# Window attention and a gated product on one core: first product block by block, differences on VectorE, doubled scores behind the second product

## The chip, the core and the metric

The kernel runs on one core of a Trainium2 chip. TensorE (PE) multiplies, VectorE (DVE), ScalarE (ACT) and GpSimd (POOL) do the rest, and SyncE's queue (SP) issues every DMA. The metric is device time in microseconds (us) for the whole program. Before the change three runs gave 546.87, 548.37 and 548.40 us, median 548.37 us.

## The reference

```python
scores = 1/sqrt(64) * q @ k.T                      # 8 batches, 8 heads, 576 positions, 64 wide
scores = where(0 <= rel < 64, scores, -1e9)        # rel = query position - key position
attn   = exp(scores - max) / (sum + 1e-9)
x      = attn @ v                                  # heads side by side: 4608 x 512
h      = x @ w_in                                  # 512 x 1024
solu   = h * softmax(h)
ln     = (solu - mean) / sqrt(var + 1e-6) * g_ln
out    = ln @ w_out                                # 1024 x 512
```

The weights w_in and w_out arrive as 64-bit floats and are turned into 32-bit ones on the chip.

## The kernel before

The 4608 tokens are 36 tiles of 128. For each tile: scores (L400, one 64x128 block per head and half tile) into the one buffer pS; softmax (L428 and L433, or L421 on a masked tile; exponential L437, sums' reciprocal L446 and L449, scaling L452); the turn of the probabilities (PE transposes L506 and copies L511 for tiles 0 to 7, by DMA through memory, pd and raw, from tile 8); values (L530, into pX, copied to xH in L538 or L540 and its remainder xL in L541); the first product (L556 or L567, into the one buffer pH); the norm (maximum L582, exponential L584, product with its sum L587, square L593, power L600, scaling L604); the turn of that (L627, yd, L637, for tiles 1 to 33); the second product (L685 or L695, into pO) and the store (L702, L703).

Tiles 0 to 2 multiply plain 32-bit numbers in the first product, tile 0 in the second as well. Later tiles take three faster passes: rounded halves wH (made by ScalarE in L333) and remainders wL (L336). For both weights the remainder of a block's first half is made by VectorE and that of the second half by GpSimd. Each weight has four blocks (rows of 128 of w_in, of 256 of w_out): names w 0 to 3 and 4 to 7. L308 to L315 decode a block, L319 scales a block of w_out.

Masks: for tiles in MASKED (1 to 5) TensorE adds the mask to the scores by a 128x512 product with an identity (L384), VectorE takes two half maxima from PSUM (L421) and ScalarE's exponential reads PSUM. Other tiles get the mask on VectorE in L428, then a maximum in L433. SCALES = 3 is the first tile whose probabilities GpSimd scales, VectorE scaling the earlier ones. From tile EARLY = 3 VectorE copies the second half of the turned probabilities.

The order is written by a planner: each step states its engine, its cost, what it reads and writes. TensorE's steps stay in the order of the loop over t (L736 on), every other engine's steps are sorted by when TensorE's plan needs them. Where the plan has a gap on TensorE it puts products of the identity (L784, "filler", into pO). The buffers' counts (RINGS) set the remaining waits: one pH, one pS, nine weight slots "w", where eight hold the blocks and the remainders take over slots of blocks no longer needed.

In the loop, tile t's first product is followed by work for tiles ahead: scores of tile t+3 up to t = 3, and from t = 4 those of t+4; at t = 4 two sets of scores stand side by side (tiles 7 and 8). Tile t-3's second product closes the step from t = 3 on.

Of the kernel before, what the change touches and what calls it, by code (L numbers as in the profile page):

```python
# [24 lines left out]
NEG = -1.0e9  # L25

AHEAD = 3
FURTHER = 4

HASTE = 1  # L30
# [1 line left out]
LOOSE = 2  # L32
BEHIND = 3

EARLY = 3

JOINS = 8

PLANES = 4

HEADS = 1
MASKED = range(1, 6)
SCALES = 3

PLAIN_IN = 3
PLAIN_OUT = 1

BY_DMA = (1, 2)
# [137 lines left out]
def tile_window_attention_solu_moe(  # L186
# [17 lines left out]
    nc = tc.nc  # L204
# [7 lines left out]
    NC = DM // P  # L212
# [63 lines left out]
    def W32(i):  # L276
        return T("w", i, [P, 2, 512])
# [52 lines left out]
    def split(i):  # L330

        for x in range(2):
            plan.op("ACT", 600, lambda x=x: nc.scalar.copy(WH(i, x), W32(i)[:, x]),  # L333
                    [("w", i), ("w", i, x), ("w", NC + 1 if i < NC else NW - 1)], [("H", i, x)])
            engine, eng, cost = (("DVE", nc.vector, 690), ("POOL", nc.gpsimd, 1450))[x]
            plan.op(engine, cost, lambda x=x, eng=eng: eng.tensor_sub(  # L336
                WL(i)[:, x], W32(i)[:, x], WH(i, x).bitcast(F32)),
                [("w", i), ("w", i, x), ("H", i, x)], [("w", NW + i, x)])
# [37 lines left out]
    def scores(t):  # L376
        first = first_of(t)

        def emit():
            q, k = Q(t), K(t)  # L380
            if t in MASKED:
                mk = masksB[first]
                for r in range(2):
                    nc.tensor.matmul(  # L384
                        PS(t)[:, r], identB,
                        bass.AP(tensor=mk.tensor, offset=mk.offset, ap=[mk.ap[0], [0, NPAIR], mk.ap[1]]),
                        start=True, stop=False)
            for p in range(NPAIR):
                for half in range(2):
                    for r in range(2):  # L390
                        rs = slice(r * D, (r + 1) * D)
                        keys = k[rs, p, :P]
                        if half or first == 0:
                            a = k[rs, p, half * P:half * P + WIN]
                            gap = 0 if first == half else P
                            if half and gap:
                                a = k[rs, p, :WIN]
                            keys = bass.AP(
                                tensor=a.tensor, offset=a.offset, ap=[a.ap[0], [gap, 2], a.ap[1]])
                        nc.tensor.matmul(  # L400
                            PS(t)[half * WIN:(half + 1) * WIN, r, p],
                            q[rs, p, half * WIN:(half + 1) * WIN], keys, start=t not in MASKED,
                            stop=t not in MASKED or p == NPAIR - 1)

        plan.op("PE", 1430 if t in MASKED else 1000, emit, [("qk", t)], [("pS", t)], loose=t < LOOSE)
# [61 lines left out]
    def soft_planes(t):  # L467
        if t < SOFT_BY_DMA:
            return
        for x in range(2):  # L470
            engine, copy, cost = ("POOL", nc.gpsimd.tensor_copy, 1050)
            plan.op(engine, cost, lambda x=x, copy=copy: copy(  # L472
                PP(t)[:, :, 4 * x:4 * x + 4].rearrange("p k h n -> p k (h n)"),
                SS(t)[:, 4 * x:4 * x + 4].rearrange("p h n -> p (h n)").bitcast(U16).rearrange("p (n k) -> p k n", k=2)),
                [("sS", t, 4 * x + i) for i in range(4)], [(*SLOT(t)[0], x)])
# [41 lines left out]
    def XH(t):  # L517
        return T("xH", t, [P, NC, P], F32 if t < PLAIN_IN else F32R)
# [27 lines left out]
    def PH(t):  # L546
        return T("pH", t, [P, DFF], pool=ps_h)
# [4 lines left out]
    def moe_in(t, h):  # L552
        hs = slice(h * 512, (h + 1) * 512)
        if t < PLAIN_IN:
            for c in range(NC):
                plan.op("PE", 930, lambda c=c: nc.tensor.matmul(  # L556
                    PH(t)[:, hs], XH(t)[:, c], W32(c)[:, h],
                    start=(c == 0), stop=(c == NC - 1)),
                    [("xH", t), ("w", c), ("w", c, h)], [("pH", t)])
            return  # L560
        passes = [(c, *k) for c in range(NC) for k in (
            (XH, WH, "xH", "H", 0), (XH, WL, "xH", "w", NW), (XL, WH, "xL", "H", 0))]
        if t == PLAIN_IN:

            passes.sort(key=lambda k: k[4] == "w")
        for n, (c, x, w, xk, wk, o) in enumerate(passes):
            plan.op("PE", 233, lambda n=n, c=c, x=x, w=w: nc.tensor.matmul(  # L567
                PH(t)[:, hs], x(t)[:, c], WH(c, h) if w is WH else WL(c)[:, h],
                start=(n == 0), stop=(n == len(passes) - 1)),
                [(xk, t), (wk, o + c, h)], [("pH", t)])  # L570
# [108 lines left out]
    def moe_out(t):  # L679
# [22 lines left out]
        plan.op("ACT", 580, lambda: nc.scalar.copy(ot(), PO()), [("pO", t)], [("ot", t)])  # L702
        plan.dma(P * DM * 4, lambda: nc.sync.dma_start(out[t * P:(t + 1) * P, :], ot()), [("ot", t)], [])  # L703

    def on(f, t, *args):
        if 0 <= t < NTILE:
            f(t, *args)

    def ahead(t):

        at = t + AHEAD + (t >= FURTHER)
        return range(at - (t == FURTHER), at + 1)

# [22 lines left out]
    for t in range(NTILE + BEHIND):  # L736
        for a in ahead(t):
            on(load, a + 1)
        on(turn, t - 1)
        if t == PLAIN_IN:  # L740
            for i in range(NC):
                split(i)
        on(moe_in, t, 0)
        if t == 0:
            scores(2)
            softmax(2)
        if t < BEHIND:
            on(moe_in, t, 1)
            on(moe_norm, t)
            on(planes, t)  # L750
            on(transposes, t + 1)
            on(scores, t + AHEAD)
            on(softmax, t + AHEAD)
            on(soft_planes, t + AHEAD)
            on(soft_turn, t + AHEAD)
            on(join, t + 1)
            on(values, t + 1)
        else:
            on(transposes, t + 1)
            on(moe_in, t, 1)  # L760
            on(moe_norm, t)
            on(planes, t)
            if t - BEHIND < NTILE - BY_DMA[1]:
                on(moe_transpose, t - BEHIND)
            on(join, t + 1)
            on(values, t + 1)
            for a in ahead(t):
                on(scores, a)
                on(softmax, a)
                on(soft_planes, a)  # L770
                on(soft_turn, a)
            if t - BEHIND == PLAIN_OUT:
                for i in range(NC, NC + NF // 2):
                    split(i)
            if t - BEHIND + 1 >= NTILE - BY_DMA[1]:
                on(moe_transpose, t - BEHIND + 1)
            on(moe_out, t - BEHIND)

    plan.first = [("qk", 0), ("raw", 0), ("v", 0), ("qk", 1), ("raw", 1), ("raw", 2), ("raw", 3), ("v", 1), ("qk", 2)]
    def filler(n):  # L780
# [53 lines left out]
```

## Time and profile before

| | |
|---|---|
| runs | 546.87, 548.37, 548.40 us |
| profiled execution | 549.3 us, span from first to last instruction 547.5 us |
| PE busy | 530.9 us (97%) |
| DVE, ACT, POOL busy | 367.4, 330.3, 292.9 us |
| mean granted TensorE clock | 0.99 of full |
| DMA | 115.58 MB, mean 211 GB/s |

How to read it: PE is busy nearly all the time, so what the other engines do counts where PE waits. The page's line of the granted clock shows nines except one eight, in a slice of some 14 us. A busy PE can also be multiplying the filler, or running at the lower clock.

### The profile page before, as it was taken

The page shows a single profiled execution, that of the slowest core. Times are in us where ns is not written, and L with a number is a line of the kernel's source. Part 1 is how long each engine was busy: PE and PEld are TensorE (multiplying, and loading weights), DVE is VectorE, ACT ScalarE, POOL GpSimd, SP SyncE. Part 2 cuts the span into 40 slices and gives each one's busy share as a digit, 9 for nine tenths or more (in the row PEclk, how much of TensorE's full clock was granted, in tenths as well). Part 3 has the DMA queues.
Part 4 walks back from the last instruction along what each step waited for, and adds up shares of the span by engine and source line. Part 5 has one row for each costly group of instructions (what it writes and reads, how often), then busy time and mean ns, then how long its engine had stood idle before and what let it go on. Part 6 is the DMA issues. An engine that isn't in the chain of part 4 may idle for free.

```text
span 547.5 us, 11649 instructions
## 1 busy us (share of the span) xinstructions
PE 530.9 (97%) x4250; PEld 416.9 (76%) x4250; DVE 367.4 (67%) x725; ACT 330.3 (60%) x955; POOL 292.9 (53%) x490
## 2 busy tenths in 40 slices
PE   8799799899999999999999999999999999999996
PEld 7565486688877877778778777777877777777885
DVE  4999758766666666666666666666666677655530
ACT  4468475576666666666666666656666666663330
POOL 5214988664555555555555555555555555671110
PEclk9999989899999999999999999999999999999999
DMA  8963115647999999999999999999999994787211
GB/s 355 403 262 116 48 59 168 209 146 208 236 255 233 242 246 237 257 234 242 241 256 231 246 261 217 243 262 222 262 243 237 246 233 155 189 235 174 59 38 38
DMA packets 153081, 115.58 MB, mean 211 GB/s; under 512 B 129856, under 2 KB 129856, under 8 KB 152512
## 3 DMA queue, kind: packets, MB, share of 16 engines
q1 hardware_dynamic: 153024, 114.84, 81.0%
q8 instruction: 33, 0.54, 0.4%
q14 instruction: 24, 0.20, 0.1%
HBM read 41.42 MB, written 41.42 MB: 151 GB/s over the span
## 4 chain that ended last, share of the span: by engine, by line
PE 84%; DVE 7%; POOL 3%; issue 2%; DMA 2%; ACT 1%; SPq 0%; POOLq 0%; ACTq 0%
PE pO L695 35%; PE pH L567 33%; PE pX L530 6%; PE pS L400 5%; DMA raw<-pd 2%; DVE w L313 1%; PE pO L685 1%; DVE w L315 1%; PE pH L556 1%; POOL e L604 1%; DVE w L309 1%; PE t L506 1%; DVE sS L452 1%; POOL w L336 1%; POOL sS L452 1%
## 5 line engine op out<-in xcount | busy, mean ns | idle before, releaser
L452 POOL TENSOR_SCALAR sS<-sS,rec 128x128 f32<-128x128 f32 x264 | 117.4, 467 | 147.1 <-DVE rec L449 144.7
L695 PE MATMUL pO<-w_outH,yH 128*128 128x512 f32 x280 | 115.3, 412 | 0.7 <-ACT ot L702 0.7
L695 PE MATMUL pO<-w,yH 128*128 128x512 f32 x280 | 111.6, 399 | 0.0
L695 PE MATMUL pO<-w_outH,yL 128*128 128x512 f32 x280 | 110.6, 395 | 0.0
L567 PE MATMUL pH<-w_inH,xH 128*128 128x512 f32 x264 | 106.5, 403 | 0.0
L567 PE MATMUL pH<-w,xH 128*128 128x512 f32 x264 | 104.2, 398 | 0.0
L567 PE MATMUL pH<-w_inH,xL 128*128 128x512 f32 x264 | 104.1, 394 | 0.0
L437 ACT ACTIVATE sS<-sS,nmx 128x128 f32<-128x128 f32 x248 | 96.2, 390 | 9.6 <-DVE nmx L433 4.7
L702 ACT COPY ot<-pO 128x512 f32<-128x512 f32 x36 | 21.1, 587 | 97.8 <-PE pO L695 77.4
L584 ACT ACTIVATE e<-pH,mst 128x1024 f32<-128x1024 f32 x36 | 40.2, 1118 | 59.1 <-DVE mst L582 58.8
L582 DVE TENSOR_REDUCE mst<-pH 128x1 f32<-128x1024 f32 x36 | 44.1, 1224 | 42.0 <-PE pH L567 42.0
L604 POOL TENSOR_SCALAR e<-e,mst 128x512 f32<-128x512 f32 x72 | 60.1, 843 | 16.8 <-DVE mst L601 14.9
L596 DVE SCALAR_TENSOR_TENSOR mst<-mst 128x1 f32<-128x1 f32 x36 | 27.8, 772 | 60.1 <-ACT pl L593 60.1
L695 PEld LDWEIGHTS pO<-w_outH,yH 128*128 128x128 f32 x280 | 52.9, 189 | 18.0 <-issue 4.8
L695 PEld LDWEIGHTS pO<-w_outH,yL 128*128 128x128 f32 x280 | 53.0, 189 | 13.2
L695 PEld LDWEIGHTS pO<-w,yH 128*128 128x128 f32 x280 | 52.9, 189 | 10.9
L567 PEld LDWEIGHTS pH<-w_inH,xH 128*128 128x128 f32 x264 | 49.9, 189 | 13.2 <-ACT sS L437 0.2
L567 PEld LDWEIGHTS pH<-w_inH,xL 128*128 128x128 f32 x264 | 50.1, 190 | 12.4
L567 PEld LDWEIGHTS pH<-w,xH 128*128 128x128 f32 x264 | 49.6, 188 | 11.4 <-issue 0.2
L472 POOL COPY raw<-sS 128x1024 uint16<-128x1024 uint16 x56 | 56.7, 1043 | 0.0
L437 ACT ACTIVATION_READ_ACCUMULATOR sS<-sS,nmx 128x1 f32 x248 | 46.6, 188 | 0.0
L663 DVE TENSOR_TENSOR yL<-yT,yH 128x512 fp32r<-128x512 f32 x66 | 44.5, 708 | 2.6 <-ACT yH L661 2.6
(95 smaller groups left out, 867.0 us busy)
## 6 DMA issues: line engine op xcount, KB each, us to landing
qk<-qk SPq DMA_DIRECT2D x36, 640.0 KB, 5.9
yd<-pl SPq DMA_DIRECT2D x33, 512.0 KB, 6.6
pd<-raw SPq DMA_DIRECT2D x28, 512.0 KB, 3.7
v<-vS SPq DMA_DIRECT2D x36, 256.0 KB, 3.4
y<-ot SPq DMA_DIRECT2D x36, 256.0 KB, 3.1
raw<-w_in SPq DMA_DIRECT2D x4, 1024.0 KB, 10.6
raw<-w_out SPq DMA_DIRECT2D x4, 1024.0 KB, 8.6
yT<-yd SPq DMA_TRANSPOSE x33, 4.8
```

Of the source, the lines that this page charges most:

```text
L400: nc.tensor.matmul(PS(t)[half * WIN:(half + 1) * WIN, r, p], q[rs, p, half * WIN:(half + 1) * WIN], keys, start=t not in MASKED, stop=t no ...
L437: plan.op("ACT", 580, lambda h=h: nc.scalar.activation(SS(t)[:, h], PS(t)[:, h // NPAIR, h % NPAIR] if t in MASKED else SS(t)[:, h], AF.Ex ...
L452: plan.op(engine, cost, lambda h=h: v.tensor_scalar(SS(t)[:, h], SS(t)[:, h], rec()[:, h:h + 1], 0.0, ALU.mult, ALU.add), [("rec", t)], [( ...
L472: plan.op(engine, cost, lambda x=x, copy=copy: copy(PP(t)[:, :, 4 * x:4 * x + 4].rearrange("p k h n -> p k (h n)"), SS(t)[:, 4 * x:4 * x + ...
L530: nc.tensor.matmul(PX(t)[r * D:(r + 1) * D, p, ks], (V if half else VX)(t)[:, h * D:(h + 1) * D], PT(t)[:, r * NPAIR + p, ks], start=True, ...
L567: plan.op("PE", 233, lambda n=n, c=c, x=x, w=w: nc.tensor.matmul(PH(t)[:, hs], x(t)[:, c], WH(c, h) if w is WH else WL(c)[:, h], start=(n ...
L582: plan.op("DVE", 1230, lambda: nc.vector.tensor_reduce(nmax(), PH(t), axis=AX.X, op=ALU.max, negate=True), [("pH", t)], [key(0)])
L584: plan.op("ACT", 1320, lambda: nc.scalar.activation(E(t), PH(t), AF.Exp, bias=nmax(), scale=1.0, accum_out=se()), [("pH", t), key(0)], H2 ...
L596: plan.op("DVE", 130, lambda: nc.vector.scalar_tensor_tensor(kk(), se(), se(), ss(), ALU.mult, ALU.mult), [key(1), key(3)], [key(5)])
L604: plan.op("POOL", 770, lambda h=h, hs=hs: nc.gpsimd.tensor_scalar(E(t)[:, hs], E(t)[:, hs], nmean(), kk(), ALU.add, ALU.mult), [key(4), ke ...
L663: plan.op("DVE", 690, lambda hs=hs: nc.vector.tensor_sub(YL(t)[:, hs], YT(t)[:, hs], YH(t)[:, hs].bitcast(F32)), [("yT", t), ("yH", t, h)] ...
L695: plan.op("PE", 233, lambda f=f, i=i, x=x, k=k, y=y, w=w: nc.tensor.matmul(PO(), y(t)[:, f], w(i, x), start=(f == k == 0), stop=(f == NF - ...
```

## The change

TensorE's first product of tile 0 takes each block of w_in for both halves of the output before the next block (WIDE = 1). The remainders of w_in are all made by VectorE; those of w_out stay shared. Tiles 2 and 3 leave MASKED, so VectorE masks them. GpSimd scales from tile 2 on. ScalarE copies both halves of the turned probabilities of tile 3 too. The scores and softmax of tiles 2 to 5 get places from a table, and the second of the doubled scores stands behind the second product. The planner's price of a plain product falls from 930 to 870.

```diff
+PLACES = {2: (0, 0), 3: (0, 2), 4: (1, 2), 5: (2, 2)}
-EARLY = 3
+EARLY = 4
-MASKED = range(1, 6)
-SCALES = 3
+MASKED = (1, 4, 5)
+SCALES = 2
+WIDE = 1
@@ split
-            engine, eng, cost = (("DVE", nc.vector, 690), ("POOL", nc.gpsimd, 1450))[x]
+            engine, eng, cost = (("DVE", nc.vector, 690), ("POOL", nc.gpsimd, 1450))[x * (i >= NC)]
@@ moe_in
+            both = t < WIDE
+            if both and h:
+                return
             for c in range(NC):
-                plan.op("PE", 930, lambda c=c: nc.tensor.matmul(
-                    PH(t)[:, hs], XH(t)[:, c], W32(c)[:, h],
+                for x in range(2) if both else (h,):
+                    plan.op("PE", 870, lambda c=c, x=x: nc.tensor.matmul(
+                        PH(t)[:, x * 512:(x + 1) * 512], XH(t)[:, c], W32(c)[:, x],
...
+    def attend(t):
+        scores(t)
+        softmax(t)
+        soft_planes(t)
+        soft_turn(t)
+    def first_tiles(t, place):
+        for a, at in PLACES.items():
+            if at == (t, place):
+                attend(a)
@@ the loop
-        if t == 0:
-            scores(2)
-            softmax(2)
         if t < BEHIND:
+            first_tiles(t, 0)
             on(moe_in, t, 1)
             on(moe_norm, t)
             on(planes, t)
+            first_tiles(t, 1)
             on(transposes, t + 1)
-            on(scores, t + AHEAD)
...
+            first_tiles(t, 2)
...
-            for a in ahead(t):
-                on(scores, a)
...
+            for a in ahead(t)[:1]:
+                on(attend, a)
...
             on(moe_out, t - BEHIND)
+            for a in ahead(t)[1:]:
+                on(attend, a)
```

TensorE's order from the middle of tile 0's first product (pH_360; w_212, w_268, w_307 and w_341 are the blocks 0 to 3 of w_in; pS_402 before and pS_414 after are tile 2's scores, t the turned probabilities of tile 1). Before:

```order
L556 MATMUL pH_360<-w_341,xH_347 128x512
L384 LDWEIGHTS identB
L384 MATMUL pS_402<-maskNoneB,identB 128x512
L384 LDWEIGHTS identB
L384 MATMUL pS_402<-maskNoneB,identB 128x512
L400 MATMUL pS_402<-qk_165 64x128 x16
L556 MATMUL pH_360<-w_212,xH_347 128x512
L556 MATMUL pH_360<-w_268,xH_347 128x512
L556 MATMUL pH_360<-w_307,xH_347 128x512
L556 MATMUL pH_360<-w_341,xH_347 128x512
L506 MATMUL t_445<-ident,sS_314 128x128 x4
L506 MATMUL t_451<-ident,sS_314 128x128 x4
```

TensorE's rows at the same place now:

```order
L563 MATMUL pH_360<-w_212,xH_347 128x512 x2
L563 MATMUL pH_360<-w_268,xH_347 128x512 x2
L799 MATMUL pO_filler<-ident 128x128 x2
L563 MATMUL pH_360<-w_307,xH_347 128x512 x2
L799 MATMUL pO_filler<-ident 128x128 x2
L563 MATMUL pH_360<-w_341,xH_347 128x512 x2
L509 MATMUL t_400<-ident,sS_314 128x128 x4
L509 MATMUL t_407<-ident,sS_314 128x128 x4
L403 MATMUL pS_414<-qk_165 64x128 x16
```

Both products of a block stand together, nothing is left of the product behind the last block, and tile 2's scores come after tile 1's turn, without the mask.

VectorE's order around the maximum of tile 2's first product (mst_726 before, mst_683 after; w_673, w_706, w_716, w_760 before and w_675, w_731, w_758, w_769 after are the remainders of blocks 0 to 3; xL is tile 3's). Before:

```order
L336 TENSOR_TENSOR w_706<-w_268,w_inH 128x512
L592 RECIPROCAL mst_609<-mst_609 128x1
L336 TENSOR_TENSOR w_716<-w_307,w_inH 128x512
L582 TENSOR_REDUCE mst_726<-pH_671 128x1
L511 COPY PT_752<-t_728 128x512
L336 TENSOR_TENSOR w_760<-w_341,w_inH 128x512
L421 TENSOR_REDUCE nmx_782<-pS_733 128x4
L587 ISA e_757,mst_726<-pH_671,e_757 128x1024
L587 ISA mst_726 128x1
L541 TENSOR_TENSOR xL_795<-pX_762,xH_790 128x512
```

VectorE's rows at the same place now:

```order
L339 TENSOR_TENSOR w_675<-w_212,w_inH 128x512
L589 TENSOR_REDUCE mst_683<-pH_627 128x1
L339 TENSOR_TENSOR w_675<-w_212,w_inH 128x512
L449 TENSOR_SCALAR rec_729<-sm_635 128x8
L339 TENSOR_TENSOR w_731<-w_268,w_inH 128x512 x2
L594 ISA e_708,mst_683<-pH_627,e_708 128x1024
L594 ISA mst_683 128x1
L544 TENSOR_TENSOR xL_745<-pX_710,xH_739 128x512
L339 TENSOR_TENSOR w_758<-w_307,w_inH 128x512 x2
L452 RECIPROCAL rec_729<-rec_729 128x8
L339 TENSOR_TENSOR w_769<-w_341,w_inH 128x512
```

VectorE's four remainders have become eight, the maximum stands behind the first of them, the copy PT of tile 3 is gone from here, and the reciprocal for tile 4's scaling (rec_729) stands behind six of the eight.

TensorE's order around tile 1's second product (pO_1137 before, pO_1080 after; pS_1079 and pS_1115 before, pS_1053 and pS_1133 after are the scores of tiles 7 and 8; pH_1155 is tile 5's first product). Before:

```order
L530 MATMUL pX_1057<-PT_1031,v_487 64x64 x2
L400 MATMUL pS_1079<-qk_638 64x128 x16
L400 MATMUL pS_1115<-qk_779 64x128 x16
L695 MATMUL pO_1137<-w_outH,yH_992 128x512
L695 MATMUL pO_1137<-w_822,yH_992 128x512
```

TensorE's rows now, at the end of that product:

```order
L702 MATMUL pO_1080<-w_outH,yH_1049 128x512
L702 MATMUL pO_1080<-w_1023,yH_1049 128x512
L702 MATMUL pO_1080<-w_outH,yL_1072 128x512
L403 MATMUL pS_1133<-qk_727 64x128 x16
L574 MATMUL pH_1155<-w_inH,xH_1070 128x512
L574 MATMUL pH_1155<-w_675,xH_1070 128x512
```

Tile 8's scores have moved from the front of the 24 products to their end.

## Rows read from the trace of the kernel before

**Rows 1.** Windows by stage: width, busy us and instructions per engine, clock, DMA

```profile
40.13:52.79 12.66, 12.10 (x106) 7.37 (x103) 12.66 (x30) 10.33 (x33) 3.79 (x9) 1.00 0.33 100
52.79:70.56 17.77, 13.76 (x100) 9.02 (x101) 14.38 (x24) 10.66 (x27) 17.49 (x20) 0.87 0.20 68
70.56:81.27 10.71, 10.71 (x107) 8.88 (x106) 5.31 (x16) 6.98 (x25) 8.79 (x14) 0.90 0.14 55
81.27:99.90 18.63, 16.71 (x145) 11.04 (x145) 17.03 (x24) 11.62 (x32) 16.84 (x27) 1.00 0.63 176
99.90:107.25 7.35, 7.35 (x25) 5.88 (x26) 5.48 (x9) 2.04 (x10) 5.60 (x7) 0.77 0.48 174
147.00:487.00 340.00, 339.30 (x2778) 270.78 (x2777) 234.35 (x456) 220.47 (x651) 195.41 (x332) 1.00 0.99 238
```

**Rows 2.** Timeline of PE: start, us, line, operands, idle before and releaser

```profile
28.13 1.12 PE L556 MATMUL pH<-w,xH 128*128 128x512 f32 x2 [0.16 <-DVE w L315]
...
34.19 1.04 PE L506 MATMUL t<-ident,sS 128*128 128x128 f32 x8
...
40.13 7.13 PE L556 MATMUL pH<-w,xH 128*128 128x512 f32 x16
...
50.62 1.60 PE L784 MATMUL pO_filler<-ident 128*128 128x128 f32 x12
...
66.51 0.37 PE L530 MATMUL pX<-PT,vx 128*64 128x64 f32 x1 [4.01 <-DVE PT L511]
...
98.79 1.10 PE L400 MATMUL pS<-qk 64*64 64x128 f32 x32 [1.92 <-DVE sS L428]
```

**Rows 3.** Chain that ended last, 53 to 65 us: start, us, what

```profile
53.68 2.20 POOL w L336
...
57.53 4.44 POOL e L604 x2
...
62.73 1.27 POOL w L336
...
64.03 0.69 DVE w L336
```

**Rows 4.** Timeline of DVE

```profile
28.23 1.66 DVE L452 TENSOR_SCALAR sS<-sS,rec 128x128 f32<-128x128 f32 x8
...
37.14 1.22 DVE L587 CUSTOM_DVE_ANT_0 e<-pH,e 128x1024 f32<-128x1024 f32 x1
...
42.58 1.28 DVE L309 TENSOR_SCALAR w<-w 128x1024 f32<-128x1024 f32 x2
...
81.34 1.23 DVE L428 SCALAR_TENSOR_TENSOR sS<-pS,maskNone 128x1024 f32<-128x1024 f32 x1 [0.81 <-PE pS L400]
...
84.22 1.21 DVE L433 TENSOR_REDUCE nmx<-sS 128x8 f32<-128x1024 f32 x1
```

**Rows 5.** Timeline of POOL

```profile
50.37 3.31 POOL L452 TENSOR_SCALAR sS<-sS,rec 128x128 f32<-128x128 f32 x8 [0.43 <-DVE rec L449]
...
70.25 1.36 POOL L319 TENSOR_SCALAR w<-w,g_sb 128x512 f32<-128x512 f32 x2
71.90 0.94 POOL L600 TENSOR_TENSOR mst<-mst,neghalf 128x1 f32<-128x1 f32 x1 [0.28 <-DVE mst L598]
...
73.51 1.52 POOL L604 TENSOR_SCALAR e<-e,mst 128x512 f32<-128x512 f32 x2
74.97 2.02 POOL L627 COPY pl<-e 128x1024 uint16<-128x1024 uint16 x2
```

**Rows 6.** Line L634, the store of the planes of y

```profile
DMA to landing us min/median/max: 2.6/6.6/7.4
```

**Rows 7.** Line L637, the turning DMA of y behind it

```profile
DMA to landing us min/median/max: 4.2/4.8/6.4
```

**Rows 8.** Line L483, the turning DMA of the probabilities, and who waited

```profile
  PE pX L530: 0.7, 1
...
DMA to landing us min/median/max: 4.4/8.2/11.1
```

More of the change, by code (lines that the diff above doesn't have):

```diff
@@ L554, in moe_in @@
         if t < PLAIN_IN:
+            both = t < WIDE
+            if both and h:
+                return
             for c in range(NC):
-                plan.op("PE", 930, lambda c=c: nc.tensor.matmul(
-                    PH(t)[:, hs], XH(t)[:, c], W32(c)[:, h],
-                    start=(c == 0), stop=(c == NC - 1)),
-                    [("xH", t), ("w", c), ("w", c, h)], [("pH", t)])
+                for x in range(2) if both else (h,):
+                    plan.op("PE", 870, lambda c=c, x=x: nc.tensor.matmul(
+                        PH(t)[:, x * 512:(x + 1) * 512], XH(t)[:, c], W32(c)[:, x],
+                        start=(c == 0), stop=(c == NC - 1)),
+                        [("xH", t), ("w", c), ("w", c, x)], [("pH", t)])
             return
@@ L750, in tile_window_attention_solu_moe @@
             on(planes, t)
+            first_tiles(t, 1)
             on(transposes, t + 1)
-            on(scores, t + AHEAD)
-            on(softmax, t + AHEAD)
-            on(soft_planes, t + AHEAD)
-            on(soft_turn, t + AHEAD)
+            first_tiles(t, 2)
             on(join, t + 1)
             on(values, t + 1)
+            first_tiles(t, 3)
         else:
+            first_tiles(t, 0)
             on(transposes, t + 1)
@@ L766, in tile_window_attention_solu_moe @@
             on(values, t + 1)
-            for a in ahead(t):
-                on(scores, a)
-                on(softmax, a)
-                on(soft_planes, a)
-                on(soft_turn, a)
+            for a in ahead(t)[:1]:
+                on(attend, a)
             if t - BEHIND == PLAIN_OUT:
```

## The prediction

> **What bounds the kernel now.** I read the windows by stage first. From 147 to 487 us TensorE is busy 339.30 of 340.00 us [rows 1]: some 25 tiles go by at TensorE's pace, and nothing that the change touches is in there, since the orders of all engines differ only up to the work around tile 9. So the change is worth what TensorE gets back before about 107 us, and each microsecond won there should reach the end. The windows between the starts of its big products show where it loses: 12.66 us with 12.10 busy, 17.77 with 13.76, 10.71 all busy but at a mean clock of 0.90, 18.63 with 16.71, 7.35 at 0.77 [rows 1]. Then I read TensorE's timeline for what ends the gaps: one of 4.01 us ends with VectorE's copy PT, one of 1.92 us with VectorE's read of the other scores (L428), because pS is a single buffer [rows 2]. Last the chain behind the long one: a GpSimd remainder of 2.20 us, its two scalings of tile 0 (4.44), another remainder (1.27), only then VectorE's own remainder at 64.03, and behind that the maximum and the copy [rows 3]. VectorE waits for GpSimd there because a remainder takes over the slot of a block whose other half GpSimd has not done. Both long gaps are followed by a lower granted clock, 0.87 and 0.90 in the windows of the first, 0.77 in that of the second [rows 1]; of the two levels, 1.2 and 2.4 GHz, the time spent at the lower one is what the change can also win.
>
> I now walk the new order stage by stage, with TensorE's starts before and after.
>
> **A, the first product of tile 0, up to that of tile 1.** The last block is ready at 28.13 as before. A plain product is 7.13 / 8 = 0.89 us [rows 2], so the two that remain end at 29.91; the four that stood behind tile 2's scores are gone. VectorE ends tile 1's scaling at 28.23 + 1.66 = 29.89 [rows 4], so the turn (1.04) and tile 2's scores (1.10) [rows 2] end at 32.05. Tile 1's product needs pH free, and in VectorE's order its reader L587 now stands behind L428 and L433 of tile 2: 1.23 + 1.21 + 1.22 [rows 4] makes 35.7. TensorE fills that time with values, tile 3's scores and filler, and ScalarE's exponential lies beside it. Tile 1's product started at 40.13 [rows 2]: won 4.4. If TensorE alone set it the win would be a microsecond more; if VectorE's mask work is 2 us late it is 2.4.
>
> **B, tile 1 to tile 2.** The same contents as before, with twelve filler records before and after; the 0.56 us of idle time (12.66 less 12.10 [rows 1]) should go, since it was L587 waiting its turn. New here: GpSimd, not VectorE, scales tile 2, eight pieces in 3.31 us [rows 5], and its reciprocal stands behind two decoding steps of block 4, so it starts near 40.9 and ends near 44.2, while TensorE wants the second four pieces at about 44.0. I charge 0.2: won 0.4, bounds 0.6 and -1.5 (the reciprocal another decoding step late).
>
> **C, tile 2 to tile 3.** Before 17.77 us. The contents are those of stage B, 12.10 us [rows 1], plus two more filler records at about 0.12 (1.60 us for twelve that overlap [rows 2]): 12.3. That removes the 4.01 us and the slow stretch behind it, if nothing takes their place. What comes late next is VectorE: from the end of tile 1's L587 (about 46.9) to that of tile 2's it has two half maxima (1.2), four one-input decoding steps (1.28 for two [rows 4], so 2.6), three two-input ones (as L428, 3.6), a maximum and the product (1.2 each), four of the eight remainders (0.69 each [rows 3], 2.8) and small ones (0.5): 13.1, ending at 60.0. TensorE, through its filler, asks at 35.7 + 12.3 + 12.3 = 60.3. The cover is thus 0.3 us thick. I charge 0.3: won 5.1, bounds 5.4 and 2.9 (VectorE's two-input steps stretched as its neighbour's were).
>
> **D, tile 3's product to tile 0's second product.** 10.71 us at a clock of 0.90 are 9.6 at full clock [rows 1], but the planner puts ten filler records in, 1.2 us, so 10.8. Then TensorE needs tile 0's scaled e for its transposes. GpSimd's list before it: tile 4's scaling from 62.4 on (the reciprocal stands behind six of the eight remainders), 3.31; the power, 0.94; a half block of w_out, 0.68, which waits for VectorE's last decoding of block 6; the two scalings, 1.52 [rows 5]. That is 68.9, 69.6 with the wait, where TensorE comes for the second half at about 69.0. I charge 0.7: lost 0.8 or 0.9 (10.71 - 11.6); bounds a gain of nothing and a loss of 3.1 (scalings at 4.44 as in [rows 3]).
>
> **E, second product of tile 0 to that of tile 1.** 18.63 us less the wait of 1.92 and the 1.10 of scores that move behind [rows 1, 2]: 15.6. The next to come late is the turned y of tile 1. GpSimd's list goes on with three half blocks (2.0), a power, two scalings and the planes (2.02 [rows 5]): about 75.3. Their store lands 2.6 to 7.4 us later, 6.6 in the middle [rows 6], so at 81.9; on SP's queue the turning DMA stands behind tile 0's output store too, which TensorE's end at 79.4 holds until about 80.4. With 4.8 us to landing (6.4 at most [rows 7]) it is there at 86.7; the product would start at 79.4 + 8.5 = 87.9 and needs ScalarE's rounding first. In the kernel before TensorE came so late that this had cover. I charge 0.8: won 2.2, bounds 3.0 and -1.0.
>
> **F, that product with tile 8's scores behind it.** 7.35 us at 0.77 are 5.7 at full clock, plus 1.10: won 0.6. L428 of tile 7 has long read pS then.
>
> The other edits (ScalarE copying both halves of tile 3, GpSimd freed of four remainders, 1.27 to 2.20 us each [rows 3], two masks gone from TensorE) are in these stages.
>
> **Sum.** 4.4 + 0.4 + 5.1 - 0.9 + 2.2 + 0.6 = 11.8 us. The profiled execution took 549.3 us, 0.9 above the median of 548.37; it would take 537.5, and the median becomes 536.6.
>
> On the port between VectorE and GpSimd: the two scalings of tile 0 took 4.44 us while VectorE ran two-input steps [rows 3], and 1.52 when it did not [rows 5]. The Trainium skill (SBUF — State Buffer, Who interferes with whom) says that a VectorE instruction with two inputs in SBUF and a GpSimd one that reads SBUF exclude each other for a whole instruction; by that rule the trace agrees, and eight differences on VectorE speak against the change. By the row the loss falls in D; by the rule it falls wherever two such steps meet, which is rival 1.
>
> **Rivals.**
> 1. GpSimd becomes the bound. VectorE's eight remainders and last decoding steps hold up its list, and the scalings of tile 0 take 4.44 instead of 1.52. For it: [rows 3], and a list from 62 to 75 us without a gap. Against it: only two or three of VectorE's two-input steps stand beside that list. TensorE waits 2.9 more in D, and a lower clock as after the old gap (10.71 less 9.6, 1.1 us) follows; the wait also gives the y turn its time back, 0.4. Gain 11.8 - 3.6 = 8.2, time 540.2.
> 2. The lead is given back at tile 8, the first whose probabilities turn by DMA. If its softmax does not come forward, TensorE waits there. The turn takes 8.2 us in the middle, and 11.1 once cost a wait of 0.7 [rows 8], so the spare is 11.1 - 0.7 - 8.2 = 2.2. Gain 2.2 at most, time 546 to 548. Against it: all that feeds tile 8 is itself released by TensorE's earlier scores.
> 3. Slower: tile 8's softmax starts one second product later on TensorE, and on SP's queue its planes' store is now behind the turning of y. If the order of those two keeps the turn late for good, every one of the 28 tiles of [rows 8] waits. At the 0.7 us seen once that is 19.6 us, less 11.8: 556.2; it decides from 11.8 / 28 = 0.42 us a tile. Against it: SP's order is the old one from its 72nd row of 241 on, and the spare of 2.2 is large against that.
>
> **How the numbers follow.** Forecast 0.60 (534.6 to 538.6), none of the charged waits 0.08 (534 to 535), rival 1 0.23, rival 2 0.05, rival 3 0.04. What this kernel's measurement can tell from no change is about 0.3%, 1.6 us. Faster: the first three and half of the second rival, 0.93; same 0.03; slower 0.04. The range takes the forecast, the case without waits and most of the first rival: 533.6 to 541.5.
>
> **What would show it.** Tile 1's product starting near 35.7 (A); no gap above 1 us on TensorE from 28 us until the tile 1 second product, and tile 3's product near 60.6 (C); GpSimd's two scalings of tile 0 ending near 69.6 (D); tile 1's second product near 88.6 with the output store issued ahead of the turning DMA (E); a granted clock of 1.00 in every window after 28 us; 13.6 us a tile (340 / 25) after that as before. Wrong would be a new gap of over 2 us with a slow clock behind it in D or E, or a wait for the turned probabilities at more than one tile.

## The result, and the profile after

The changed kernel took 540.35 us (median of four runs, 540.31 to 540.61); the kernel before took 547.62 us on the same chip (546.84 to 548.40). The ratio is 0.986 with a 95% interval of 0.9826 to 0.9894: faster by 7.3 us, where 11.8 were forecast. The time lies in the range (533.6 to 541.5), 3.75 us above the forecast and next to the 540.2 of the first rival. The profiled execution took 540.3 us, its span 538.4 after 547.5. From here the changed kernel's lines are meant: scaling of the probabilities L455, first product L563 and L574, second L692 and L702, scores L403, first reader of the scores (with the mask) L431.

The windows by stage of the changed kernel, cut at the same starts of TensorE as [rows 1], with the same columns and one more ahead, from where tile 0's product goes on to tile 1's (the cut at 63.00 lies 0.15 us behind the start of tile 3's product in TensorE's timeline, 62.85):

```profile
28.31:36.03 7.72, 7.72 (x121) 5.87 (x121) 6.67 (x15) 4.93 (x13) 1.22 (x2) 1.00 1.01 388
36.03:50.38 14.35, 13.05 (x103) 7.34 (x102) 12.99 (x23) 10.02 (x35) 7.58 (x12) 1.00 0.22 71
50.38:63.00 12.62, 12.60 (x107) 7.68 (x105) 12.60 (x20) 10.23 (x30) 12.40 (x13) 1.00 0.31 106
63.00:76.01 13.01, 11.93 (x116) 9.11 (x115) 11.48 (x27) 8.08 (x27) 11.08 (x18) 1.00 0.09 29
76.01:91.75 15.74, 15.74 (x117) 10.24 (x113) 12.71 (x21) 13.31 (x36) 15.61 (x21) 1.00 0.47 143
91.75:98.70 6.95, 6.95 (x57) 5.20 (x57) 6.88 (x12) 1.08 (x4) 6.21 (x12) 1.00 0.86 245
140.00:480.00 340.00, 340.00 (x2781) 271.38 (x2780) 235.00 (x454) 221.17 (x653) 195.54 (x335) 1.00 0.97 237
```

The 17.77 us stage is 12.62, the granted clock is 1.00 in each window, and the end of the last stage has come forward from 107.25 to 98.70: 8.55 of the 9.1 us by which the span is shorter. Two stages are longer than before, the second (14.35 after 12.66) and the fourth (13.01 after 10.71). TensorE's waits between 20 and 140 us (us in total, times, longest) say for what:

```profile
PE t L509 <- POOL sS L455: 1.9, 3, 1.0
PE pH L563 <- DVE w L318: 1.5, 1, 1.5
PE t L664 <- POOL e L611: 0.4, 1, 0.4
```

The second line is a wait at 25.91 us for a decoded block of w_in, which the kernel before had too (2.10 us at 25.74). New are waits for GpSimd's scaled probabilities and its scaled e. Where they stand is in TensorE's timeline:

```profile
45.46 0.33 PE L509 MATMUL t<-ident,sS 128*128 128x128 f32 x1 [0.26 <-POOL sS L455]
46.77 0.33 PE L509 MATMUL t<-ident,sS 128*128 128x128 f32 x1 [0.98 <-POOL sS L455]
50.38 7.13 PE L563 MATMUL pH<-w,xH 128*128 128x512 f32 x16
...
68.67 1.02 PE L509 MATMUL t<-ident,sS 128*128 128x128 f32 x3 [0.66 <-POOL sS L455]
...
73.30 0.66 PE L664 MATMUL t<-ident,e 128*128 128x128 f32 x4 [0.37 <-POOL e L611]
...
76.01 7.13 PE L692 MATMUL pO<-w,yH 128*128 128x512 f32 x16
...
90.64 1.10 PE L403 MATMUL pS<-qk 64*64 64x128 f32 x32
```

The first two belong to tile 2's turn, the third to tile 4's, the last to tile 0's second product. No row is left of the 4.01 and 1.92 us of [rows 2]. GpSimd's timeline shows the scalings of tiles 2, 3 and 4 (three groups of eight) and that of e, beside the 3.31 and 1.52 of [rows 5]:

```profile
41.24 5.47 POOL L455 TENSOR_SCALAR sS<-sS,rec 128x128 f32<-128x128 f32 x8 [6.68 <-DVE rec L452]
50.19 8.22 POOL L455 TENSOR_SCALAR sS<-sS,rec 128x128 f32<-128x128 f32 x8
...
64.58 4.73 POOL L455 TENSOR_SCALAR sS<-sS,rec 128x128 f32<-128x128 f32 x8 [1.56 <-DVE rec L452]
70.70 2.55 POOL L611 TENSOR_SCALAR e<-e,mst 128x512 f32<-128x512 f32 x2 [0.19 <-DVE mst L608]
```

Of these 24 scalings the view of the tile from 40 to 76 us gives the durations in ns (min/median/max):

```profile
L455 POOL TENSOR_SCALAR sS<-sS,rec x24: 363/368/1852, 41.2 to 68.9; 128x128 f32<-128x128 f32 x24
```

Thirteen take 0.36 or 0.37 us, the other eleven 0.73 to 1.85: a piece either runs undisturbed or is held up. VectorE's timeline has, beside tile 2's eight, two steps that read two operands from SBUF (L318 and L316, decoding w_out), and beside tile 4's two remainders (L339) and one decoding step (L318, 67.16):

```profile
40.84 0.20 DVE L452 RECIPROCAL rec<-rec 128x8 f32<-128x8 f32 x1
...
41.51 1.22 DVE L318 SCALAR_TENSOR_TENSOR w<-raw,w 128x1024 int32<-128x1024 int32 x1
...
44.31 0.86 DVE L314 TENSOR_SCALAR w<-w 128x1024 int32<-128x1024 int32 x1
45.21 1.27 DVE L316 SCALAR_TENSOR_TENSOR w<-raw,w 128x1024 int32<-128x1024 int32 x1
...
64.37 0.69 DVE L339 TENSOR_TENSOR w<-w,w_inH 128x512 fp32r<-128x512 f32 x1
...
65.23 0.68 DVE L339 TENSOR_TENSOR w<-w,w_inH 128x512 fp32r<-128x512 f32 x1
...
67.16 1.21 DVE L318 SCALAR_TENSOR_TENSOR w<-raw,w 128x1024 int32<-128x1024 int32 x1
```

GpSimd's timeline in narrow windows, one piece at a time, shows the three long ones among tile 2's eight:

```profile
41.24 1.64 POOL L455 TENSOR_SCALAR sS<-sS,rec 128x128 f32<-128x128 f32 x1 [6.68 <-DVE rec L452]
...
44.60 0.80 POOL L455 TENSOR_SCALAR sS<-sS,rec 128x128 f32<-128x128 f32 x1
...
45.38 1.33 POOL L455 TENSOR_SCALAR sS<-sS,rec 128x128 f32<-128x128 f32 x1
```

The first is 1.27 us longer than the median, beside L318's 1.22. The last is 0.96 longer, beside L316; the one between is 0.43 longer, mostly beside L314, a decoding step with one input. Eight medians are 8 x 0.368 = 2.94 us; with the 1.22 and 1.27 of the two-input steps that is 5.43, and the group took 5.47. This sum has L316 whole and leaves L314 out, so it agrees more closely than its parts do. For tile 4 it is 2.94 + 0.68 (one of the two L339) + 1.21 = 4.83, measured 4.73. For tile 3 it is 2.94 + 1.49 (L318) + 1.21 + 1.24 (two L316) + 0.68 (L339) = 7.56, measured 8.22, with one-input decoding steps beside it too. So far this is arithmetic on one trace; the first experiment tests it. The Trainium skill (SBUF — State Buffer, Who interferes with whom) says that a VectorE instruction with two inputs in SBUF and a GpSimd one that reads SBUF shut each other out for a whole instruction; the 1.27 us beside 1.22 agree.

### The profile page after: what moved, and what is told of

The parts are those of the page before. It is cut to its first block, busy times and chain, and to the rows that moved or that the text cites. A ratio compares the mean times of both kernels' runs of the same rounds, so it can differ in the third digit from the quotient of the medians.

```text
span 538.4 us, 11611 instructions
## 1 busy us (share of the span) xinstructions
PE 527.8 (98%) x4236; PEld 412.1 (77%) x4236; DVE 372.1 (69%) x716; ACT 330.4 (61%) x956; POOL 294.9 (55%) x494
## 4 chain that ended last, share of the span: by engine, by line
PE 87%; DVE 7%; POOL 2%; issue 2%; ACT 1%; POOLq 0%; ACTq 0%; DVEq 0%
PE pO L702 37%; PE pH L574 33%; PE pS L403 6%; PE pX L533 6%; POOL sS L455 2%; DVE w L316 1%; PE pO L692 1%; DVE w L312 1%; DVE w L339 1%; PE pH L563 1%; DVE w L318 1%; PE t L509 1%; PE pO_filler L799 1%; DVE w L314 1%; POOL e L611 0%
## 5 line engine op out<-in xcount | busy, mean ns | idle before, releaser
L455 POOL TENSOR_SCALAR sS<-sS,rec 128x128 f32<-128x128 f32 x272 | 128.4, 490 | 142.7 <-DVE rec L452 132.5
L702 PE MATMUL pO<-w_outH,yH 128*128 128x512 f32 x280 | 114.7, 410 | 0.7 <-ACT ot L709 0.7
L702 PE MATMUL pO<-w,yH 128*128 128x512 f32 x280 | 111.0, 396 | 0.0
L440 ACT ACTIVATE sS<-sS,nmx 128x128 f32<-128x128 f32 x264 | 102.5, 390 | 13.6 <-DVE nmx L436 6.8
L702 PE MATMUL pO<-w_outH,yL 128*128 128x512 f32 x280 | 110.1, 393 | 0.0
L574 PE MATMUL pH<-w_inH,xH 128*128 128x512 f32 x264 | 105.9, 401 | 0.0
L574 PE MATMUL pH<-w,xH 128*128 128x512 f32 x264 | 104.2, 398 | 0.0
L574 PE MATMUL pH<-w_inH,xL 128*128 128x512 f32 x264 | 103.7, 393 | 0.0
L611 POOL TENSOR_SCALAR e<-e,mst 128x512 f32<-128x512 f32 x72 | 58.5, 820 | 16.1 <-DVE mst L608 13.4
L702 PEld LDWEIGHTS pO<-w_outH,yH 128*128 128x128 f32 x280 | 52.5, 187 | 17.9 <-issue 4.8
L702 PEld LDWEIGHTS pO<-w_outH,yL 128*128 128x128 f32 x280 | 52.6, 188 | 13.3 <-DVE yL L670 0.3
L702 PEld LDWEIGHTS pO<-w,yH 128*128 128x128 f32 x280 | 52.6, 188 | 10.8
L574 PEld LDWEIGHTS pH<-w_inH,xH 128*128 128x128 f32 x264 | 49.5, 188 | 13.1 <-ACT sS L440 0.2
L574 PEld LDWEIGHTS pH<-w_inH,xL 128*128 128x128 f32 x264 | 49.6, 188 | 12.5
L574 PEld LDWEIGHTS pH<-w,xH 128*128 128x128 f32 x264 | 49.6, 188 | 11.4 <-issue 0.2
L440 ACT ACTIVATION_READ_ACCUMULATOR sS<-sS,nmx 128x1 f32 x264 | 49.6, 188 | 0.0
L670 DVE TENSOR_TENSOR yL<-yT,yH 128x512 fp32r<-128x512 f32 x66 | 46.9, 743 | 1.7 <-ACT yH L668 1.7
```

Source lines behind the costliest of these rows:

```text
L440: plan.op("ACT", 580, lambda h=h: nc.scalar.activation(SS(t)[:, h], PS(t)[:, h // NPAIR, h % NPAIR] if t in MASKED else SS(t)[:, h], AF.Ex ...
L455: plan.op(engine, cost, lambda h=h: v.tensor_scalar(SS(t)[:, h], SS(t)[:, h], rec()[:, h:h + 1], 0.0, ALU.mult, ALU.add), [("rec", t)], [( ...
L611: plan.op("POOL", 770, lambda h=h, hs=hs: nc.gpsimd.tensor_scalar(E(t)[:, hs], E(t)[:, hs], nmean(), kk(), ALU.add, ALU.mult), [key(4), ke ...
L670: plan.op("DVE", 690, lambda hs=hs: nc.vector.tensor_sub(YL(t)[:, hs], YT(t)[:, hs], YH(t)[:, hs].bitcast(F32)), [("yT", t), ("yH", t, h)] ...
L702: plan.op("PE", 233, lambda f=f, i=i, x=x, k=k, y=y, w=w: nc.tensor.matmul(PO(), y(t)[:, f], w(i, x), start=(f == k == 0), stop=(f == NF - ...
```

## The experiments

The theory: the miss against the forecast lies in GpSimd's scalings of tiles 2 and 4, which lose up to the whole length of each two-input VectorE step beside them. The rival: the scalings are late because their reciprocals are, GpSimd having sat idle 6.68 us until L452. Kernels were sent in four groups, each group on one chip with runs of the kernel before, whose median was 547.25, 547.49, 548.39 and 546.97 us. Where one is set beside the changed kernel's 540.35, the two ran in different groups, so the ratio to before stands with each.

**The two-input steps replaced.** In the changed kernel, for blocks of w_out:

```diff
-        plan.op("DVE", 1240, ... scalar_tensor_tensor(t(), hi(), -0x40000000, t(), ...))   # L316
-        plan.op("DVE", 1240, ... scalar_tensor_tensor(t(), lo(), 29, t(), ...))            # L318
+            for k in range(2):
+                plan.op("DVE", 1240, ... tensor_reduce(junk[:, k:k + 1], block, op=ALU.max))
```

> The changed kernel (540.35 us), where the two decoding steps of each block of w_out that read two inputs from SBUF are replaced by two maxima over the block of the same length (one input), so the weights of the second product are not the true ones. The order on every engine and the load of VectorE stay. Theory 1 (GpSimd's scaling of tiles 2, 3 and 4 was stretched by VectorE's two-input steps beside it): the eight pieces of tile 2, 5.47 us in the changed kernel, fall to 2.8 to 3.3, TensorE's waits of 0.26 and 0.98 for them go, tile 2's product starts near 48.5 instead of 50.4, and the time falls by 1.5 to 2.5, to about 538.3. Theory 2 (GpSimd was late because the reciprocal stands late in VectorE's order): the pieces keep 5.5 us or the wait stays, and the time is within 0.4 of 540.35.

Measured: 537.20 us (536.97 to 537.41), ratio 0.9795 (0.9764 to 0.9825). The order is the same, and so is the replaced steps' length (1.21 us at 41.71). GpSimd's timeline of this kernel, where the scaling is L461 and e's is L617:

```profile
41.44 3.03 POOL L461 TENSOR_SCALAR sS<-sS,rec 128x128 f32<-128x128 f32 x8 [6.68 <-DVE rec L458]
49.02 4.70 POOL L461 TENSOR_SCALAR sS<-sS,rec 128x128 f32<-128x128 f32 x8 [0.96 <-DVE rec L458]
63.22 3.66 POOL L461 TENSOR_SCALAR sS<-sS,rec 128x128 f32<-128x128 f32 x8 [2.78 <-DVE rec L458]
68.27 1.52 POOL L617 TENSOR_SCALAR e<-e,mst 128x512 f32<-128x512 f32 x2 [0.18 <-DVE mst L614]
```

The idle time before tile 2's scaling is 6.68 us as before, the reciprocal just as late; the eight pieces take 3.03 instead of 5.47, those of tile 4 3.66 instead of 4.73, those of e 1.52 instead of 2.55. No wait of TensorE for them is left. The theory stands and the rival falls. The time is 3.15 us below the changed kernel's, and in the traces nearly all of that is won by tile 0's second product (72.96 after 76.01). From tile 1's product to tile 2's it is now 12.07 us (36.23 to 48.30) where the forecast had 12.3, and from tile 3's to tile 0's second 11.7 (61.26 to 72.96) where it had 11.6. In between the next gap shows: TensorE waits 0.64 us for VectorE in front of tile 3's product. It is not a version to use, since it takes out decoding.

Tile 3's eight still take 4.70 us, well over 2.94, and no two-input step is left beside them. VectorE's timeline of this kernel has there, besides the maxima, the one-input decoding steps:

```profile
50.71 0.69 DVE L312 TENSOR_SCALAR w<-w 128x1024 f32<-128x1024 f32 x1
...
52.11 1.38 DVE L314 TENSOR_SCALAR w<-w 128x1024 int32<-128x1024 int32 x2
```

The pieces beside these last 0.80 to 1.32 us, those beside a maximum (49.39, 1.22) 0.37. So the two-input steps are the larger part of what holds GpSimd up, but not all of it. The replaced steps wrote a block and the maxima do not; that it is not the writing shows in the kernel before, where the step shown next writes as much to SBUF beside undisturbed pieces (0.38 us) of the 3.31 of [rows 5]:

```profile
51.43 1.21 DVE L587 CUSTOM_DVE_ANT_0 e<-pH,e 128x1024 f32<-128x1024 f32 x1
```

**Tile 2 scaled by VectorE again.**

```diff
-SCALES = 2
+SCALES = 3
```

> The changed kernel with SCALES = 3, so VectorE scales tile 2 again (1.66 us for eight pieces of tile 1). Theory 1: TensorE's waits for GpSimd in tile 1's stage go (1.24 us and some stretched transposes), but VectorE has 1.7 us more in front of tile 0's L318 and tile 2's product; 540.35 less 0.5 to 1.5. Rival (VectorE is the bound there and the scaling only moved): VectorE passes its 1.7 us on, 540.35 plus 0 to 1.5.

Measured: 541.52 us (540.70 to 541.88), ratio 0.9871 (0.9839 to 0.9904). Tile 2's product starts at 48.49 instead of 50.38, and TensorE's waits are then:

```profile
PE pH L574 <- ACT w_inH L336: 2.7, 1, 2.7
...
PE pO L702 <- ACT yH L668: 1.3, 1, 1.3
```

The 1.9 us won at tile 2 are lost at tile 3, whose rounded blocks of w_in come late from ScalarE. Removing the wait without adding to another engine's load helps (the first experiment); with the scaling handed to VectorE the time is not told from the changed kernel's.

**Tile 2, or tiles 2 and 4, scaled by ScalarE.**

```diff
+        if t in (2,):          # second kernel: (2, 4)
+            for h in range(H):
+                plan.op("ACT", 390, lambda h=h: nc.scalar.mul(SS(t)[:, h], SS(t)[:, h], rec()[:, h:h + 1]), ...)
+            return
```

> The changed kernel with tile 2's probabilities scaled by ScalarE instead of GpSimd. Theory 1 (the scaling was stretched by VectorE's two-input steps on a port that ScalarE does not share): eight pieces in about 3.2 us, TensorE's waits of 1.24 us in tile 1's stage go, tile 2's product starts near 48.5, and the time is 1 to 2.5 us below 540.35. Rival (ScalarE, busy 10 of 14 us in that stage, passes the 3.2 us on to tile 1's exponential or to the rounded w_in): 540.35 or up to 1.5 more.

> As the last one, and tile 4's probabilities scaled by ScalarE too, so GpSimd reaches tile 0's two scalings earlier. Theory 1: another 0.5 to 1 us below the last one. Rival (ScalarE late with the rounded w_in and the turned y): 0 to 2 us above it.

Measured: 542.93 us (542.52 to 544.97), ratio 0.9913 (0.9879 to 0.9948), and 546.87 us (546.38 to 548.84), ratio 0.9993 (0.9972 to 1.0014). In the first, ScalarE's timeline has the eight pieces in 2.45 us, undisturbed:

```profile
41.32 2.45 ACT L456 ACTIVATE sS<-sS,rec 128x128 f32<-128x128 f32 x8 [0.96 <-DVE rec L452]
```

Tile 2's product starts at 48.98, 1.4 earlier, but the planner sorts the rest anew and three waits of 0.7 to 1.1 us follow before 140 us. The longest is for GpSimd's scaled e, which now falls beside two-input steps itself (VectorE's L318 at 70.91 and L316 at 72.04; GpSimd's timeline):

```profile
69.67 4.05 POOL L616 TENSOR_SCALAR e<-e,mst 128x512 f32<-128x512 f32 x2 [0.38 <-ACT PT L519]
```

The profiled execution is also the slowest of the six (544.97), with a single wait of 1.6 us for turned probabilities at 341 us; whether the other five have it is not known. In the second the largest wait of TensorE is this one:

```profile
PE pO L707 <- DVE yL L675: 3.0, 1, 3.0
```

Neither beats the changed kernel. The scalings could be moved off GpSimd, but the contention moved on to e and the time did not follow.

**The remainders shared again.**

```diff
-            engine, eng, cost = (("DVE", ...), ("POOL", ...))[x * (i >= NC)]
+            engine, eng, cost = (("DVE", ...), ("POOL", ...))[x]
```

> The changed kernel with the remainders of w_in shared between VectorE and GpSimd as before. Theory (these four remainders on GpSimd are what held up the copy PT and with it TensorE for 4 us): the gap in front of tile 3's product comes back in part, 3 to 6 us slower than 540.35, and TensorE's clock falls behind it. Rival (the gap went because of the earlier start and the changed places, and the split only shifts work): within 1 us of 540.35.

Measured: 544.85 us (543.80 to 546.83), ratio 0.9954 (0.9928 to 0.9979). The 4.5 us that it costs are of the size that the theory gave, but the old gap of 4 us does not come back; TensorE's waits are instead these:

```profile
PE t L509 <- POOL sS L455: 2.3, 3, 1.0
...
PE pH L574 <- DVE mst L594: 1.5, 1, 1.5
PE pO L702 <- ACT yH L668: 1.4, 1, 1.4
PE pO L702 <- DVE yL L670: 0.7, 1, 0.7
```

Tile 2's eight scalings take 5.47 us here too, so VectorE's eight remainders are not what stretched them.

**The remainders alone, in the kernel before.** The same line there, `[x * (i >= NC)]` in place of `[x]`.

> The kernel before with only the remainders of w_in all on VectorE. Theory (GpSimd's remainders hold the slots and with them VectorE's maximum and copy PT): the gap of 4.01 us and the low clock behind it go, 4 to 6 us faster than the kernel before. Rival (VectorE has 2.8 us more in front of the same copy, so the gap stays in another form): 0 to 2 us.

Measured: 544.93 us (542.97 to 546.57), ratio 0.9944 (0.9917 to 0.9971). TensorE's timeline:

```profile
65.73 0.27 PE L530 MATMUL pX<-PT,vx 128*64 128x64 f32 x1 [1.30 <-DVE PT L511]
...
96.54 1.10 PE L400 MATMUL pS<-qk 64*64 64x128 f32 x32 [2.70 <-DVE sS L428]
```

The gap of 4.01 us is 1.30, as the chain of [rows 3] has it, but the wait for pS behind it grows from 1.92 to 2.70 and tile 1's product starts later (41.57 after 40.13).

**Block by block undone, and alone.**

```diff
-WIDE = 1
+WIDE = 0                                   # in the changed kernel
...
+            both = t < WIDE                # in the kernel before, WIDE = 1, with the new loop
```

> The changed kernel with WIDE = 0: tile 0's first product by halves, four products of 0.89 us behind the last block and tile 2's scores between the halves. Theory (the 4.1 us won up to tile 1's product come from this and last to the end): 540.35 plus 2.5 to 4. Rival (VectorE and GpSimd, not TensorE, set the time of tiles 2 and 3, so the early start is given back there): plus 0 to 1.

> The kernel before with only tile 0's first product block by block. Theory (tile 1's product starts 3 to 4 us earlier, but the chain through GpSimd in front of tile 3's product does not move, so the gap there grows by what was won): 0 to 1 us faster than the kernel before. Rival (the lead lasts): 3 to 4 us faster.

Measured: undone 541.32 us (540.63 to 541.94), ratio 0.987 (0.9837 to 0.9902); alone 547.18 us (545.69 to 548.53), ratio 0.9986 (0.9964 to 1.0008). (Alone, the planner keeps its old price of 930.) Undone, tile 1's and tile 2's products start 2.9 and 4.3 us later (38.97, 54.68), tile 0's second product only 1.8 (77.85), and the time is up by 1.0. Alone, tile 1's product starts at 39.06, 1.1 earlier, and tile 2's waits for it:

```profile
52.77 7.11 PE L561 MATMUL pH<-w,xH 128*128 128x512 f32 x16 [1.63 <-DVE mst L592]
```

Of a lead of 2.9 us in the first stages the next ones give back 1.1 by the traces and 1.9 by the medians, as the rival has it for VectorE and GpSimd; alone the edit is not told from none.

**The doubled scores undone, and alone.**

```diff
-            for a in ahead(t)[:1]:         # undone in the changed kernel; alone, the same lines the other way
+            for a in ahead(t):
...
-            for a in ahead(t)[1:]:
-                on(attend, a)
```

> The changed kernel with the second of the doubled scores (tile 8) in front of tile 1's second product again. Theory: the wait for L428 and the lower clock behind it come back, 1.9 + 1.7 less what the wait spares later; 540.35 plus 2.5 to 4. Rival (the turned y of tile 1 would have ended the wait there anyway, the two waits overlap): plus 0 to 1.

> The kernel before with only the second of the doubled scores moved behind tile 1's second product. Theory: the 1.92 us gap and the slow stretch behind it go, 2.5 to 3.5 us faster than the kernel before of the same chip. Rival (a wait for the turned y or for pS takes its place): 0 to 1 us.

Measured: undone 544.34 us (542.11 to 545.25), ratio 0.9935 (0.991 to 0.996); alone 545.47 us (543.88 to 547.35), ratio 0.9954 (0.9928 to 0.998). TensorE's timeline of the first brings the wait back, in the size of [rows 2]:

```profile
93.65 1.35 PE L403 MATMUL pS<-qk 64*64 64x128 f32 x32 [1.94 <-DVE sS L431]
...
95.95 0.63 PE L702 MATMUL pO<-w_outH,yL 128*128 128x512 f32 x1
```

Undone it costs 4.0 us: the wait, and products behind it at the lower clock (0.63 us each instead of 0.40; the granted clock is 0.81 from 91.71 to 100.60). Alone it wins 2.0, with the 4 us gap still ahead of it.

**Masks on TensorE again for tiles 2 and 3.**

```diff
-MASKED = (1, 4, 5)
+MASKED = range(1, 6)
```

> The changed kernel with tiles 2 and 3 masked on TensorE again, as before: VectorE has about 1.9 us less between 40 and 65, TensorE about 1.0 us more. Theory (it is VectorE's two-input work beside GpSimd that costs stages B and D, and the mask is not part of it): the eight scalings of tile 2 stay at 4.5 to 5.5 us, and the time is 340.35 + 200 = 540.4 us, plus 0 to 1.0 for TensorE's extra work. Rival (VectorE is short of time in those stages, whatever it does): tile 2's product starts up to 1 us earlier and the time falls by 0.5 to 1.5 us, to 539 to 540 us.

Measured: 539.39 us (538.95 to 539.96), ratio 0.986 (0.9824 to 0.9896). The time is the rival's, but not by its way: tile 2's product starts later, not earlier (52.31), since the planner sets tile 1's back to 38.90. TensorE's and GpSimd's timelines:

```profile
38.90 7.13 PE L563 MATMUL pH<-w,xH 128*128 128x512 f32 x16
45.87 1.86 PE L509 MATMUL t<-ident,sS 128*128 128x128 f32 x8
```

```profile
40.49 6.86 POOL L455 TENSOR_SCALAR sS<-sS,rec 128x128 f32<-128x128 f32 x8
```

The scaling takes even 6.86 us, yet TensorE, which comes later for it, waits for none of it; tile 0's second product starts at 74.97, 1.0 us before the changed kernel's. By the ratios, 0.986 and 0.986, this kernel is not told from the changed one: no run shows that moving these masks to VectorE wins anything, and what VectorE's time is worth stays open.

**A price of the planner nearer to the trace.**

```diff
-        engine, v, cost = ("POOL", nc.gpsimd, 400) if t >= SCALES else ("DVE", nc.vector, 170)
+        engine, v, cost = ("POOL", nc.gpsimd, 650 if t < 5 else 400) if t >= SCALES else ("DVE", nc.vector, 170)
```

> The changed kernel with one price of its planner altered: a scaling on GpSimd is priced at 650 instead of 400 ns for tiles below 5, near the mean of 684 ns that the trace of the changed kernel shows for tile 2's eight. No work is added or removed. Theory (the order was made with a price that is too low for this stretch, so transposes were set where their scaling was late): waits of TensorE for scaled probabilities (1.9 us in sum) fall below 1 us, and the time falls by 0.5 to 2 us, to 538.4 to 539.9 us. Rival (the late scaling is the contention itself, and another order only moves the wait to the next product): same time within 0.5 us, or up to 3 us more if the planner pushes other work behind a product.

Measured: 538.91 us (538.68 to 539.52), ratio 0.9853 (0.981 to 0.9896), span 537.1 us. TensorE's waits and GpSimd's timeline (tiles 2 and 4):

```profile
PE pH L574 <- ACT pl L600: 1.3, 1, 1.3
PE t L509 <- POOL sS L455: 0.8, 1, 0.8
```

```profile
41.12 5.47 POOL L455 TENSOR_SCALAR sS<-sS,rec 128x128 f32<-128x128 f32 x8 [6.69 <-DVE rec L452]
...
63.07 3.34 POOL L455 TENSOR_SCALAR sS<-sS,rec 128x128 f32<-128x128 f32 x8
```

The time is within what the theory gave, and the waits for scaled probabilities fall from 1.9 to 0.8 us. But tile 2's scaling is as long as ever and its product starts at 50.26, 0.1 earlier: there the rival was right. The win is at tile 4, whose scaling now runs ahead of a two-input step of VectorE and takes 3.34 instead of 4.73; tile 0's second product starts at 74.75 instead of 76.01. It is the lowest time of a kernel that does the whole computation. Its four runs lie below the changed kernel's four, but in another group; by the ratios to before the two intervals overlap, so that it beats the changed kernel rests on the trace (span 1.3 us shorter, 1.26 of it at this place).

## Why the prediction was right where it was, and where it failed

- **The bound** was right: what TensorE loses before about 107 us. Of the 9.1 us of span, 8.55 are won there; the steady part is 340.00 of 340.00 us busy. The page of the kernel before has two eights in its line of the granted clock and not one, in the slices from 68 and from 96 us, each behind one of the two gaps.
- **A** was right: tile 1's product predicted at 35.7, measured 36.03, won 4.1 of 4.4. What the lead is worth at the end was overrated: undone it costs 1.0 us.
- **B failed.** Predicted +0.4, measured -1.7 (14.35 us after 12.66), at the lower bound given and 0.2 beyond. The term is "eight pieces in 3.31 us", charged 0.2 for a late start. The start was right (40.9 predicted, 41.24 measured), the duration was not: 5.47, because 3.31 came from a place in [rows 5] where the only large two-input VectorE step (L315, from 53.43) reaches the last 0.25 us, while here the order put L318 and L316 there. The mechanism was in the text, priced only for e in stage D.
- **C** was right: +5.1 predicted, 17.77 - 12.62 = 5.15 measured, tile 3's product 12.62 us after tile 2's (12.6 predicted; 12.47 by the start in the timeline). The thin cover held: VectorE is busy 12.60 of those 12.62 us.
- **D** was mis-sized by the same term: predicted -0.9, measured -2.3. Tile 4's scaling took 4.73, not 3.31, and e's 2.55, not 1.52, ending at 73.25 after a predicted 69.6, of which 2.4 is the lead lost in B. TensorE's two waits there are 0.66 and 0.37; the first experiment removes them together with those of B.
- **E** was pessimistic: predicted +2.2, measured 18.63 - 15.74 = 2.9. The queue's order came as said, the output's store at 83.79 ahead of the turning DMA at 84.22, but TensorE was busy throughout and no wait for the turned y is left. GpSimd's list was summed from 68.9, though the text had just reached 69.6, to 75.3; it ended at 79.43.
- **F** was right: +0.4 measured, +0.6 predicted. Undoing it shows the size of the wait and of the slow products behind it.
- **The sum**: 4.1 - 1.7 + 5.1 - 2.3 + 2.9 + 0.4 = 8.5 instead of 11.8. B and D are 3.5 us short, E gives 0.7 back, A and F lose 0.5. The span is 9.1 us shorter, 0.55 of it later. The forecast also took 0.9 us off for the distance of the profiled execution from its median; the changed kernel's (540.31) lies at its median, so these 0.9 are a part of the 3.75.
- **The rivals.** The first named the right engine, the right contention and nearly the right time (540.2). Its price was put on the scalings of e in D with a slow clock behind; instead most of it fell in B, on the probabilities, and the clock stayed at 1.00. That its loss of 3.6 us meets the 3.5 of B and D is luck: 2.9 + 1.1 - 0.4 in D there, 2.1 in B and 1.4 in D here. The second and third are ruled out: no wait for probabilities turned by DMA is left.
- **The parts don't add.** Alone they win 2.0 (doubled scores), 2.5 (remainders) and 0.3 us, 4.8 in all; undone they cost 4.0, 4.5 and 1.0, 9.5 in all. Behind each gap stands the next, so an early one pays only when the later ones go too. The table of places, EARLY and the price of 870 were not undone by themselves; their share stays open.

## What to carry to other kernels

Price a run of small GpSimd steps by what stands beside it in the new order: its undisturbed duration plus, as an estimate, the whole length of each VectorE step with two SBUF operands that falls in (5.43 for a measured 5.47, 4.83 for 4.73 here). Look for fast one-input steps over large blocks too: with them beside it the sum was short (7.56 for 8.22). Take the duration from a row with the same neighbours, or bound it with that sum. Ask of each gap removed whether the next engine in line has its work ready; if not, much of the lead is lost: of 2.9 us block by block kept 1.0 by the medians, 1.8 by the traces.

## What was not expected

- A scaling of 128x128 is not slowed a little, it is held up: 13 of 24 take 0.37 us at most, the others 0.73 to 1.85. With the two-input decoding steps replaced, the eight of tile 2 take 3.03 us instead of 5.47.
- Runs of the kernel before spread over 4.6 to 4.9 us in each of the four groups (545.33 to 550.04 in one of 31), the four of the changed kernel over 0.3, the four of the version without two-input decoding of w_out over 0.4. The versions with the remainders or the doubled scores put back spread over 3 us (10 runs each). No run here shows why.
